# Products of the identity in TensorE's first waits, and another order of the first weight conversions

## The chip, the cores and the metric

The kernel runs on one NeuronCore of one Trainium2 chip. The time is the device time of one execution in microseconds (us), as the median of several executions. TensorE (PE) multiplies matrices, ScalarE (ACT) and VectorE (DVE) work on elements, GpSimd (POOL) does some of that and issues some transfers, and SyncE (SP) issues most transfers. Each engine has its own queue; they wait for one another by semaphores.

## What is computed

A gated linear attention is followed by a bilinear feed-forward layer, all in fp32:

```
f = 1/(1+exp(-f_logit))                            # 4 batches, 8 heads, 768 steps, 48 wide
state = f[t] * state + outer(k[t], v[t])           # per batch and head
y[t] = q[t] @ state
x = y as (3072 tokens, 384)
out = ((x @ w_a) * (x @ w_b)) @ w_out              # w_a, w_b: 384 x 1536; w_out: 1536 x 384
```

The weights come as 64-bit floats, of which the kernel makes 32-bit ones on the chip.

## The kernel before, in words

**Tiling.** The tokens are cut into 8 blocks of 384. A block needs two *units* of attention (four heads each, over the block's tokens), so units 0 and 1 make block 0, units 2 and 3 make block 1. A unit passes through these steps, each a function of the kernel: `front_parts` (sigmoids on ACT, an affine step on POOL, running products on DVE, and the multiplication of k and q by them, L306 to L333), `turn` and `turned` (transposes of k on PE, L411, and their copy out of PSUM on ACT, L418 or L420), `scores` (L387) and `mask` (L400, DVE), `gains` (L435) and `carried` (L462 and L464: the states are added up on DVE), `hand_on` (L473: the last state is scaled for the next half), `within` (L484) and `across` (L510), which add both parts of y up in PSUM, and `y_of`: `out_of_bank` copies y out of PSUM in three parts (L529), and `stored` moves it by small transfers into the block's `xT` (L549).

**Feed-forward.** For the first two blocks, `up(blk, i)` multiplies one 128-wide tile of w_b and then of w_a by the block (L593: three products for each, into two PSUM banks). I call this a *tile pair*, and its halves b and a. `product` copies b out on ACT (L613) and multiplies it by a on DVE (L615), which gives both banks back. There are four such banks, `ps_f`, handed out in turn by the list `idle`. So a tile pair can start only when the product before the last one has been taken out. After 24 tile pairs come the products with w_out (L808), and for later blocks other forms of the same (L715); these last stages are written out by a planner from estimated durations.

**Weights.** `load_weights` loads piece after piece (SP); pieces 2j and 2j+1 hold two tiles of w_b and of w_a (pieces 0, 1, 12 and 13 one tile; 14 to 19 are w_out). `begin` and `end` convert them by a generator in three steps: two ACT operations and one on POOL (L58, L59, L60), two more on ACT (L62, L63), and one plus one on DVE (L68, L73; the latter three times, once for each 128 rows, for w_a and w_b). `begin(n)` carries pieces up to n through the ACT steps, `begin(n + 0.5)` only the first of these for one more piece; `end(n)` carries them through all. `needed(i)` says how many pieces tile i needs; tile 7 needs pieces 8 and 9.

**Order.** Everything before the planner is written out by hand, in the function's text, in the order in which each engine's queue then has it. Each engine takes its own instructions in that order. The text goes through units 0 and 1, block 0's first tile pairs mixed with units 2 and 3, and then a loop over `ups`, which mixes the two blocks' tile pairs and converts one more piece with each. The planner begins with the last of these tile pairs, and puts the attention of unit 4 and later beside the main work.

Of the kernel before, what the change touches and what calls it, by code (L numbers as in the profile page):

```python
# [136 lines left out]
def by_quotients(ctx, tc, q, k, f_logit, v, moe_w_a, moe_w_b, moe_w_out, out, ident, weights, bad):  # L137
    nc = tc.nc
# [3 lines left out]
    NKT, NFT, DM = w_ba.shape[2], w_out.shape[1], out.shape[1]  # L142
    NH = S // BLK
    NQ = H // 4
    NC = BLK // C
    NJ = BLK // SUB
# [5 lines left out]
    FIRST = range(NQ)  # L152
# [46 lines left out]
    def load_unit(u, names="fkqv"):  # L199
        for do in loads_of(u, names):  # L200
            do()
# [37 lines left out]
    def load_weights(n=1):  # L239
        for _ in range(n):  # L240
            if len(raws) == len(todo):
                return
            dst, src, (k, m) = todo[len(raws)]
            raw = dst
            if src.dtype != FP32:

                if len(raws) in EARLY:
                    raw = groups[:, EARLY.index(len(raws))].bitcast(mybir.dt.uint64)
                else:
                    raw = next(raw_places)  # L250
                raw = raw[:, 0:k * m].rearrange("p (k m) -> p k m", k=k)
            nc.sync.dma_start(out=raw, in_=src)
            raws.append(raw)

    def begin(n):

        while 2 * n > begun[0] < 2 * len(todo):
            i, second = divmod(begun[0], 2)
            dst, src, shape = todo[i]
            if not second:  # L260
                going.append(
                    from_double(
                        nc, dst, raws[i], shape[0], next(blocks), bits[i % len(bits)], sign, whole, shape[0] == NKT
                    )
                    if src.dtype != FP32 else iter(())
                )
            next(going[i], None)
            begun[0] += 1

    def end(n):  # L270

        while ended[0] < min(n, len(todo)):
            begin(ended[0] + 1)
            next(going[ended[0]], None)
            ended[0] += 1
            if ended[0] > 2 and ended[0] - 1 not in EARLY:
                load_weights()
# [15 lines left out]
    def halves(x):  # L293
        return x.rearrange("p n s -> p (n s)")
# [56 lines left out]
    ps_f = [ps_a.tile([128, 512], FP32, tag=f"ps_f{i}", name=f"ps_f{i}") for i in range(4)]  # L351
    idle = list(range(4))
# [14 lines left out]
    def home(u):  # L367

        return ps_y if u in (1, 3) else ps_x
# [25 lines left out]
    def mask(u):  # L395

        at = sb1.tile([128, 2, BLK], FP32, tag="at", name="at")
        to, x = (y.rearrange("s h (o t) -> s h o t", t=SUB) for y in (at, home(u)[:, :, 0:BLK]))
        tri = causal.unsqueeze(1).unsqueeze(1)
        nc.vector.tensor_tensor(to, x, tri.broadcast_to((128, 2, 2 * NC, SUB)), ALU.mult)  # L400
        live[u]["at"] = at

    def turn(u):

        kf = halves(sets[u % NSET]["k"])
        live.setdefault(u, {})["kT"] = sb1.tile([128, 2, NC, 128], FP32, tag="kT", name="kT")
        ps = live[u]["turned"] = [ps_f[idle.pop(0)] for _ in range(2)] if u in FIRST else pair_of(away(u))
        for n in range(2):
            for c in range(NC):
                o = n * BLK + c * C  # L410
                nc.tensor.transpose(ps[n][:, c * C:c * C + C], kf[:, o:o + C], ident)  # L411
# [10 lines left out]
    def gains(u, chunks=range(NC)):  # L422

        _, half, _ = unit(u)
        t, kT = sets[u % NSET], live[u]["kT"]
        last = half == NH - 1
        ps = live[u]["turned"]
        for n in range(2):
            for c in chunks:
                for p in range(2):  # L430
                    if last and c == NC - 1 and p == 1:
                        continue
                    for h in range(2):
                        r = slice(SUB * p, SUB * p + SUB)
                        nc.tensor.matmul(  # L435
                            ps[p][R * h:R * h + D, (n * NC + c) * D:(n * NC + c) * D + D],
                            lhsT=kT[r, n, c, R * h:R * h + D],
                            rhs=t["v"][r, n, c, h * D:h * D + D],
                            start=True,
                            stop=True,  # L440
                        )
        if chunks[0]:
            return
        st = sb3.tile([128, NJ, 2, D], FP32, tag="st", name="st")
        before = live[u - NQ]["st"][NJ] if half else None
        live[u]["st"] = [before] + [st[:, j] for j in range(NJ - 1 if last else NJ)]

    def carried(u, js=range(NJ)):

        for j in js:  # L450
            if j + 1 < len(live[u]["st"]):
                carry(u, j)
        if js[-1] == NJ - 1:
            give_back(live[u]["turned"])
# [11 lines left out]
    def hand_on(u):  # L466

        if unit(u)[1] == NH - 1:
            return
        before = live[u]["st"][-1]  # L470
        for n in range(2):
            end = products_of_f[u][:, n, BLK - 1:BLK]
            nc.vector.tensor_scalar(before[:, n], before[:, n], end, math.exp(-MIDDLE), ALU.mult, ALU.mult)  # L473
# [45 lines left out]
    def out_of_bank(u, part):  # L519

        if not part:
            if u == NQ - 1:

                live[u]["y_sb"] = groups[:, 2 * NTG - 1, PIECE:].rearrange("r (o p m) -> r o p m", p=2, m=SUB)
            else:
                live[u]["y_sb"] = sb1.tile([128, 2 * NC, 2, SUB], FP32, tag="y", name="y")
        p, e, r, rows = ((0, 0, 0, 128), (1, R, 0, D), (1, 0, R, D))[part]
        copy = nc.vector.tensor_copy if u in FIRST and p else nc.scalar.copy
        copy(live[u]["y_sb"][r:r + rows, :, p], live[u]["y"][p][e:e + rows, 0:BLK].rearrange("r (o m) -> r o m", m=SUB))  # L529

    def stored(u):
# [49 lines left out]
    def up(blk, ft):  # L581

        for _, _, _, do, *args in up_steps(blk, ft):
            do(*args)
# [22 lines left out]
    def product():  # L607

        if not factors:
            return  # L610
        blk, ft, ps = factors.pop(0)
        b_sb = next(b_copies)
        nc.scalar.copy(b_sb, ps["b"][:, 0:BLK])  # L613
        a, b = (x.rearrange("p (g t) -> p g t", g=NTG) for x in (ps["a"][:, 0:BLK], b_sb))
        nc.vector.tensor_tensor(products(blk)[:, :, ft], a, b, ALU.mult)  # L615
        give_back(ps.values())
# [321 lines left out]
    with tc.manual_schedule():  # L938
# [11 lines left out]
        def emit_all(steps):  # L950
            for _, _, do, *args in steps:
                do(*args)

        def y_of(u):
            for part in range(3):
                out_of_bank(u, part)
            stored(u)
# [16 lines left out]
        for _ in range(3):  # L974
            next(fronts[0])
        begin(1)
        turn(0)
        turned(0)
        scores(0)
        begin(2)  # L980
        gains(0)
        for _ in range(3):
            next(fronts[1])
        turn(1)
# [15 lines left out]
        within(1)  # L1000
        gains(1, range(NC - 1, NC))
        across(0)
        carried(1, range(1, 5))
        for u in FIRST:
            if u:
                across(u)
# [3 lines left out]
            stored(u)  # L1010
        begin(3)
        end(2)
        for u in FIRST:
            carried(u, range(5, NJ))
        emit_all([*scans, *others[0]])


        load_unit(3, "f")
        load_unit(2, "v")
        load_weights()  # L1020
        load_unit(3, "k")
        load_unit(3, "q")
        load_unit(3, "v")
        load_weights()
        up(0, 0)
        emit_all(others[1])
        begin(4)
        next(fronts[3])
        end(4)
        for u in FIRST:  # L1030
            hand_on(u)
        turn(2)
        scores(2)
        load_unit(4, "f")
        up(0, 1)
        mask(2)
        product()
        turned(2)
        begin(5)
# [3 lines left out]
        gains(2)  # L1043
        product()
        carried(2)
        begin(6)
        up(0, 2)
        across(2)
        end(5)
# [2 lines left out]
        y_of(2)  # L1052
        load_weights(2)
        product()
        up(0, 3)
        turn(3)
        turned(3)
        scores(3)
        begin(7)
        mask(3)  # L1060
        up(0, 4)
        product()
        begin(8)
        within(3)
        gains(3)
        carried(3)
        product()
        end(7)
        begin(9)
        end(8)  # L1070
        across(3)
        y_of(3)


        ups = [(0, 5), (0, 6)]
        for i in range(7, NFT):
            ups += [(1, i - 7), (0, i)]
        ups += [(1, i) for i in range(NFT - 7, NFT)]
        alone = len(todo) - 6
        for n, (blk, i) in enumerate(ups[0:alone]):  # L1080
            convert(needed(i))
            up(blk, i)
            end(7 + n)
            product()
            begin(ended[0] + 2)
            if 2 < n < 2 + 2 * NSET and n % 2:
                load_unit(NSET + n // 2, "kqv" if n == 3 else "fkqv")
# [523 lines left out]
```

## Time and profile before

| | |
|---|---|
| runs | 606.65, 605.12, 606.56 us; median 606.56 us |
| profiled execution | 605.75 us, of which the span from first to last instruction is 604.0 us |
| mean granted TensorE clock | 0.987 |
| PE busy | 571.5 us (95%) |
| DVE busy | 412.9 us (68%) |
| ACT busy | 267.9 us (44%) |
| POOL busy | 76.6 us (13%) |

Busy shares are of the span. A plain fp32 product stands as two matmul records in the trace, a transpose as one; a record's duration includes the time in which it runs beside its neighbours, so the spacing of starts is the better measure of speed. The granted clock is the share of full speed that the throttle let TensorE have. Waits are named by the engine that ended them.

### The profile page before, as it was taken

What the parts mean: (1) busy time and instruction counts of PE and PEld (TensorE: products, weight loads), DVE (VectorE), ACT (ScalarE), POOL (GpSimd) and SP (SyncE); (2) the same over time, 40 slices, a digit from 0 to 9 for tenths busy, and PEclk for the clock granted to TensorE, in tenths of its full rate; (3) what the DMA queues carried; (4) which work ended last, traced back from release to release, by engine and by line L of the source; (5) the groups of instructions that cost most, each with busy time, mean ns of one, the idle gap of its engine ahead of it and who ended that gap; (6) DMA issues with size and microseconds to landing.
All of it is one profiled execution on the core that took longest, in us unless ns stands there. A gap on an engine that the chain in (4) does not pass through costs nothing.

```text
span 604.0 us, 13895 instructions
## 1 busy us (share of the span) xinstructions
PE 571.5 (95%) x5778; PEld 512.5 (85%) x5778; DVE 412.9 (68%) x788; ACT 267.9 (44%) x505; POOL 76.6 (13%) x71
## 2 busy tenths in 40 slices
PE   1689799999999999999999999999999999999995
PEld 1546455557899999999989999999999999999995
DVE  6897444589968778967895768846775165746741
ACT  6476878963232455326521354326331335134300
POOL 6252433534200000000000000000000000000000
PEclk9979799999999999999999999999999999999999
DMA  9695579159743333045003420022001100000000
GB/s 207 186 276 158 186 206 297 71 90 173 142 126 105 84 77 67 2 105 119 3 1 84 117 51 2 1 78 68 2 2 47 47 0 1 2 27 0 1 29 31
DMA packets 33272, 49.42 MB, mean 82 GB/s; under 512 B 3952, under 2 KB 24976, under 8 KB 33200
## 3 DMA queue, kind: packets, MB, share of 16 engines
q1 hardware_dynamic: 30000, 42.38, 25.9%
q0 software_dynamic: 3056, 5.92, 5.8%
q8 instruction: 47, 0.77, 0.6%
q14 instruction: 25, 0.20, 0.1%
q10 hardware_dynamic: 144, 0.15, 0.1%
HBM read 33.23 MB, written 4.72 MB: 63 GB/s over the span
## 4 chain that ended last, share of the span: by engine, by line
PE 87%; DVE 7%; issue 2%; ACT 2%; DMA 1%; SPq 0%; DVEq 0%; ACTq 0%
PE ps_f L715 35%; PE ps_f L808 28%; PE ps_f L593 16%; PE ps_y L484 2%; PE ps_x L387 2%; PE ps_y L510 2%; PE ps_x L411 1%; PE ps_x L435 1%; DVE inv L329 1%; DVE sums L707 1%; DVE groups L707 1%; DVE groups L316 1%; DMA f_in<-in_f_logit_dram 1%; DVE q_in L333 1%; DMA xT<-y 1%
## 5 line engine op out<-in xcount | busy, mean ns | idle before, releaser
L593 PE MATMUL ps_f<-xT,w_ba 128*128 128x384 f32 x288 | 101.2, 511 | 6.9 <-DMA xT<-y 4.7
L593 PEld LDWEIGHTS ps_f<-xT,w_ba 128*128 128x128 f32 x288 | 56.3, 199 | 47.0 <-issue 9.5
L1259 ACT COPY sums<-ps_f 128x384 f32<-128x384 f32 x120 | 57.5, 480 | 75.9 <-PE ps_f L715 68.2
L1259 ACT COPY groups<-ps_f 128x384 f32<-128x384 f32 x120 | 57.7, 481 | 62.9 <-PE ps_f L715 39.9
L715 PE MATMUL ps_f<-xT,w_ba 128*128 128x192 f32 x384 | 78.4, 327 | 0.0
L715 PEld LDWEIGHTS ps_f<-xT,w_ba 128*128 128x128 f32 x384 | 64.8, 190 | 0.2
L715 PE MATMUL ps_f<-groups,w_ba 128*128 128x192 f32 x288 | 55.5, 327 | 0.0
L715 PE MATMUL ps_f<-x_sums,raw 128*128 128x192 f32 x288 | 54.0, 331 | 1.2 <-DVE groups L707 0.9
L808 PE MATMUL ps_f<-w_out,sums 128*128 128x192 f32 x288 | 52.2, 329 | 0.0
L808 PE MATMUL ps_f<-w_out,groups 128*128 128x192 f32 x288 | 51.7, 328 | 0.0
L715 PEld LDWEIGHTS ps_f<-x_sums,raw 128*128 128x128 f32 x288 | 46.9, 190 | 4.3 <-DVE groups L707 1.8
L808 PE MATMUL ps_f<-spare,sums 128*128 128x192 f32 x288 | 49.0, 326 | 0.0
L715 PEld LDWEIGHTS ps_f<-groups,w_ba 128*128 128x128 f32 x288 | 47.9, 190 | 0.5 <-ACT groups L1259 0.3
L808 PEld LDWEIGHTS ps_f<-w_out,sums 128*128 128x128 f32 x288 | 47.1, 190 | 0.8 <-DVE o L843 0.3
L808 PEld LDWEIGHTS ps_f<-w_out,groups 128*128 128x128 f32 x288 | 47.1, 190 | 0.7
L808 PEld LDWEIGHTS ps_f<-spare,sums 128*128 128x128 f32 x288 | 47.1, 190 | 0.1
L60 POOL TENSOR_SCALAR sums<-sums 128x768 f32<-128x768 f32 (+1 forms) x20 | 39.9, 1994 | 53.6 <-ACT sums L58 53.6
L312 POOL TENSOR_SCALAR inv<-inv 128x768 f32<-128x768 f32 x14 | 12.8, 912 | 266.7 <-ACT inv L309 266.6
L707 DVE TENSOR_TENSOR sums<-sums,groups 128x768 f32<-128x768 f32 x36 | 34.7, 965 | 14.2 <-ACT groups L1259 13.7
L707 DVE TENSOR_TENSOR sums<-ps_f,sums 128x384 f32<-128x384 f32 x60 | 32.8, 553 | 16.5 <-PE ps_f L715 15.0
L715 PE MATMUL ps_f<-x_sums,w_ba 128*128 128x192 f32 x192 | 39.3, 327 | 0.5 <-DVE sums L707 0.5
L715 PE MATMUL ps_f<-xT,raw 128*128 128x192 f32 x192 | 39.4, 328 | 0.0
(135 smaller groups left out, 857.9 us busy)
## 6 DMA issues: line engine op xcount, KB each, us to landing
raw<-w_ba POOLq DMA_DIRECT2D x11, 512.0 KB, 8.0
k_in<-in_k_dram SPq DMA_DIRECT2D x32, 144.0 KB, 3.9
q_in<-in_q_dram SPq DMA_DIRECT2D x32, 144.0 KB, 4.4
v_in<-in_v_dram SPq DMA_DIRECT2D x16, 288.0 KB, 5.0
raw<-in_moe_w_out_dram SPq DMA_DIRECT2D x6, 768.0 KB, 6.3
out_dram<-o SPq DMA_DIRECT2D x24, 192.0 KB, 1.9
f_in<-in_f_logit_dram SPq DMA_DIRECT2D x28, 144.0 KB, 3.1
xT<-y SPq DMA_DIRECT2D x45, 72.0 KB, 2.2
```

What stands on the lines that cost most here:

```text
L60: nc.gpsimd.tensor_scalar(h, h, HI_MAX, None, ALU.min)
L312: nc.gpsimd.tensor_scalar(inv, inv, EXP_K, 1.0, ALU.mult, ALU.add)
L316: nc.vector.tensor_tensor_scan(F[:, c], F[:, c], none, math.exp(MIDDLE), ALU.mult, ALU.add)
L329: nc.vector.tensor_tensor_scan(inv[:, w], inv[:, w], none[:, 0:C], first, ALU.mult, ALU.add)
L387: nc.tensor.matmul(ps[h][SUB * p:SUB * p + SUB, o:o + SUB], lhsT=kf[r, tokens(n, c, p)], rhs=qf[r, tokens(n, c, p)], start=True, stop=True,)
L484: nc.tensor.matmul(ps[p][e:e + D, o:o + SUB], lhsT=t["v"][r, n, c, h * D:h * D + D], rhs=at[r, h, o:o + SUB], start=o == 0, stop=True, ski ...
L510: nc.tensor.matmul(ps[p][e:e + D, o:o + SUB], lhsT=st[j][r, n], rhs=qf[r, tokens(n, c, p)], start=False, stop=True, skip_group_check=True,)
L593: nc.tensor.matmul(ps[nm][:, 0:BLK], lhsT=w[:, kt, ft * 128:ft * 128 + 128], rhs=xT[blk][:, kt], start=kt == 0, stop=kt == NKT - 1,)
L707: nc.vector.tensor_tensor(to, x, y, op)
L715: nc.tensor.matmul(ps[:, g], lhsT=sums_of_w[name][:, g, 128 * j:128 * j + 128], rhs=sums_of_x[blk][name], start=start and g == 0, stop=Tru ...
L808: nc.tensor.matmul(to, lhsT=x[:, i // 2, i % 2], rhs=w[:, NI * (i % 2) + i // 2], start=start and i == 0, stop=i == HFT - 1, skip_group_ch ...
L1259: do(*args)
```

## The change

Four things change.

1. A new function `keep_up(n)` makes n products of the identity with itself, 128 x 128, into the PSUM bank that stands last in `idle`. Nobody reads them. They stand on TensorE's queue three times: 9 before unit 0's transposes, 12 after unit 0's `gains`, and 30 before block 0's first tile pair.
2. Unit 0's second and third part of y are copied by ACT and no longer by DVE; unit 1's stay on DVE. DVE adds up the last states of units 0 and 1, and does the second of unit 2's first running products, before unit 1's copies and no longer after them.
3. Loads and conversions come in another order at units 2 and 3: pieces 4 and 5 are loaded earlier, unit 3's v later; `mask(2)` comes before `hand_on`; the first ACT steps of pieces 6, 7 and 8 come before ACT work that stood ahead of them or follow it more closely.
4. Tile pair (0, 4) still comes before `within(3)`, but (0, 5), which was the loop's first, now stands between `gains(3)` and `across(3)`. The loop over `ups` goes (0, 6), (0, 7), (1, 0), (0, 8), (1, 1) and so on, where it went (0, 5), (0, 6), (1, 0), (0, 7), (1, 1); the planner gets the last four tile pairs where it had five.

```diff
-        copy = nc.vector.tensor_copy if u in FIRST and p else nc.scalar.copy
+        copy = nc.vector.tensor_copy if u == NQ - 1 and p else nc.scalar.copy
...
+        def keep_up(n):
+
+            for _ in range(n):
+                nc.tensor.matmul(ps_f[idle[-1]][:, 0:128], lhsT=ident, rhs=ident, start=True, stop=True)
...
         begin(1)
+        keep_up(9)
         turn(0)
...
         gains(0)
+        keep_up(12)
         for _ in range(3):
             next(fronts[1])
...
         across(0)
-        carried(1, range(1, 5))
+        carried(1, range(1, NJ))
+        carried(0, range(5, NJ))
+        emit_all(scans)
...
         end(2)
-        for u in FIRST:
-            carried(u, range(5, NJ))
-        emit_all([*scans, *others[0]])
+        emit_all(others[0])
 
         load_unit(3, "f")
+        load_weights()
         load_unit(2, "v")
         load_weights()
         load_unit(3, "k")
         load_unit(3, "q")
-        load_unit(3, "v")
-        load_weights()
+        keep_up(30)
         up(0, 0)
         emit_all(others[1])
         begin(4)
         next(fronts[3])
+        end(3)
+        load_unit(3, "v")
         end(4)
-        for u in FIRST:
-            hand_on(u)
         turn(2)
         scores(2)
         load_unit(4, "f")
         up(0, 1)
         mask(2)
+        for u in FIRST:
+            hand_on(u)
         product()
...
-        begin(6)
+        begin(6.5)
         up(0, 2)
         across(2)
...
         product()
+        begin(7.5)
         up(0, 3)
         turn(3)
         turned(3)
         scores(3)
-        begin(7)
+        end(7)
         mask(3)
-        up(0, 4)
         product()
         begin(8)
+        up(0, 4)
         within(3)
         gains(3)
+        end(8)
         carried(3)
         product()
-        end(7)
-        begin(9)
-        end(8)
+        begin(8.5)
+        up(0, 5)
         across(3)
         y_of(3)
+        begin(9)
+        product()
 
-        ups = [(0, 5), (0, 6)]
-        for i in range(7, NFT):
-            ups += [(1, i - 7), (0, i)]
-        ups += [(1, i) for i in range(NFT - 7, NFT)]
+        ups = [(0, 6), (0, 7)]
+        for i in range(8, NFT):
+            ups += [(1, i - 8), (0, i)]
+        ups += [(1, i) for i in range(NFT - 8, NFT)]
...
             up(blk, i)
-            end(7 + n)
+            end(8 + n)
             product()
```

## The prediction

> **What bounds the kernel.** I read the page's busy times and slices first.
>
> ```profile
> PE 571.5 (95%) x5778; PEld 512.5 (85%) x5778; DVE 412.9 (68%) x788; ACT 267.9 (44%) x505; POOL 76.6 (13%) x71
> ...
> PE   1689799999999999999999999999999999999995
> ...
> PEclk9979799999999999999999999999999999999999
> ```
>
> PE is the bound, and what it loses lies ahead of 70 us: of 32.5 us idle, and the clock's two dips. Next, PE's waits up to 110 us:
>
> ```profile
> PE ps_f L411 <- DVE k_in L333: 15.0, 2, 12.5
> PE ps_f L593 <- DMA xT<-y: 4.7, 1, 4.7
> PE ps_f L593 <- DVE w_ba L73: 2.2, 1, 2.2
> PE ps_y L510 <- DVE st L464: 1.5, 2, 1.2
> ```
>
> Then PE's timeline (start, us, what):
>
> ```profile
> 12.49 1.51 PE L411 MATMUL ps_f<-ident,k_in 128*128 128x128 f32 x6 [12.49 <-DVE k_in L333]
> ...
> 33.11 7.24 PE L593 MATMUL ps_f<-xT,w_ba 128*128 128x384 f32 x12 [4.74 <-DMA xT<-y]
> 40.19 0.82 PE L411 MATMUL ps_y<-ident,k_in 128*128 128x128 f32 x6
> 40.94 0.93 PE L387 MATMUL ps_x<-q_in,k_in 48*64 48x64 f32 x48
> 41.79 4.14 PE L593 MATMUL ps_f<-xT,w_ba 128*128 128x384 f32 x12
> ...
> 64.67 1.16 PE L510 MATMUL ps_y<-q_in,st 48*48 48x64 f32 x48 [1.22 <-DVE st L464]
> ```
>
> The same tile pair takes 7.24 us after the wait and 4.14 later; the transposes 1.51 and 0.82. So PE runs at half speed up to about 25.5 us, from 33 to 39, and after 68. The clock row shows no dip before 30, but the durations do (L484 changes pace at 25.5). The windows agree for the later two (granted clock: third column from the right):
>
> ```profile
> 33.20:40.20 7.00, 7.00 (x13) 3.43 (x14) 6.83 (x12) 5.87 (x9) 3.92 (x3) 0.57 1.02 277
> 63.40:68.00 4.60, 1.22 (x52) 0.92 (x49) 3.36 (x9) 4.57 (x7) 2.84 (x2) 0.84 0.78 262
> 68.00:74.60 6.60, 6.60 (x13) 3.65 (x14) 2.39 (x6) 5.01 (x9) 1.91 (x2) 0.60 0.21 61
> ```
>
> After 70 PE waits for nothing over 1 us, so whatever is gained before stays, unless a new wait takes it back. ACT can: it needs 3.57 us a piece and works without a gap for long stretches.
>
> ```profile
> 80.96 0.90 ACT L58 ACTIVATE sums<-raw 128x768 f32<-128x768 f32 x1
> 81.76 0.99 ACT L59 ACTIVATE spare<-raw,whole 128x768 f32<-128x768 uint32 x1
> 82.65 0.90 ACT L62 ACTIVATE spare<-raw 128x768 bf16<-128x768 f32 x1
> 83.58 1.07 ACT L63 ACTIVATE spare<-spare 128x768 uint16<-128x768 bf16 x1
> 84.53 0.88 ACT L58 ACTIVATE sums<-raw 128x768 f32<-128x768 f32 x1
> ```
>
> [...]windows of 1 us put the dips at 32.4 to 39.2 and 66.5 to 73.3, 6.8 us each[...].
>
> **The change, part by part.**
>
> *Price of an identity product.* The trace has none. A plain fp32 product is two records; a 384-wide record at full speed follows every 0.3225 us (0.64 at half), and a 128-wide transpose record every 0.109 (0.213). I take 2 x 0.109 = 0.218 us, at half speed 0.427. Below, one record's 0.109; above, 0.427.
>
> *9 and 12 products.* The identity is built on POOL at 10.34 us. 9 x 0.427 = 3.84 puts the first transposes from 12.49 to at most 14.3. Scores and gains then end at 17.9 (16.45 before), and 12 products take 2.6 us at full and 5.1 at half speed: unit 1's transposes start between 19.0 (as before) and 21.6 by when the clock rises[...]. Behind them wait ACT's copies of kT and unit 2's sigmoid, which ended at 22.86 and is wanted by DVE at 24.58 (slack 1.7), and `mask(1)` at 23.38, whose scores ended at 22.03 (1.35). A delay of up to 1.7 costs nothing, more costs up to 0.4. Faster PE takes away DVE's 0.52 us wait for the gains at 26.05. `across(1)` ends between 27.8 and 28.7; I take 28.3 (28.37 before).
>
> *30 products.* 30 x 0.218 = 6.54: they end at 34.9. The first tile pair waited for xT until 33.11; xT comes 0.5 earlier or up to 0.3 later, hidden behind the products, which overshoot by 1.8. What they buy: 4.07 instead of 7.08 us for tile pair (0, 0) (41.79 to 45.86, against 33.11 to 40.19).
>
> *Unit 0's copies on ACT, DVE's order.* ACT gets 2 x 0.48 us, in its wait of 0.97 for unit 1 (if that were gone, y(1) would be as much later, still behind the 30 products); DVE loses 1.14 and fills its waits of 0.34 and 0.31 with 1.5 us of sums and scan. It reaches unit 2's reciprocal at 30.7, not 32.53, so k and q are ready at 34.6 and 35.5, pieces 2 and 3 by 39.7. PE wants them at 38.9 and 42.5: no wait. The store DMAs are the same; SP's begin 0.6 earlier.
>
> *Loads.* Pieces 4 and 5 are issued around 32.5 and 33.5 and land in 6.4 and 8.5 us: 39 and 42, wanted by ACT at 40 and 44.6. They come behind the xT transfers on SP. Unit 2's v (5.0) lands by 38, wanted at 44.5; unit 3's k and q by 41, wanted at 51; its v behind piece 6, wanted at 62. POOL's queue is unchanged. Nothing. If piece 4 came 1 us late, (0, 3) would, by as much.
>
> *Up to across(3).* Six tile pairs at 4.07 are 24.4. Attention, from starts in the trace: 1.60 + 1.34 + 0.82 + 1.60 + 1.4 + 1.0 = 7.8. DVE, chained from 39.7 on (mask 0.9, hand_on 0.65, product 0.5, scans 4.75, product 0.5, states 1.35, piece 4 1.65, k and q 1.75, piece 5), lets half a of (0, 3) start at 53.6 for 52.9: 0.8. 34.9 + 24.4 + 7.8 + 0.8 = 67.9. The waits of 1.22 and 2.17 and the second dip's 2.65 us are gone, since (0, 5) covers the state sums, pieces 6 and 7 are ready at 55.7 and 60.1, and PE stays busy. Before, the same work was done at 74.6: 6.7 us ahead.
>
> *What is late next.* (0, 6) ends at 71.8. (0, 7) now follows at once, and needs piece 8, which DVE takes in hand only behind the product of (0, 6): 0.3 + 0.56 + 0.55 + 0.4 makes PE wait 2.0 to 2.1, to 73.8. Half a needs piece 9: on ACT, y(3) (68.1 to 69.5), the rest of piece 8 (1.9), two product copies (0.8), piece 9 (3.6) end at 75.8, plus DVE 0.4: 76.3, a wait of 0.6. (1, 0) ends at 82.1. (0, 8) needs the banks of (0, 7), whose copy stands on ACT behind pieces 10 and 11: 75.8 + 7.1 + 0.45 = 83.4, a wait of 1.3. So (0, 8) starts at 83.4. Before, it would follow the same nine tile pairs at 68.0 + 6.6 + 3 x 3.87 = 86.2. **Gain 2.8 us.** After that ACT has slack: it catches up, by its 1.3 us gaps between product copies.
>
> *Clock after the new wait.* [...] I charge 0.2 (0 to 1.5).
>
> *The planner's part.* With the loop one tile pair longer, combining w_out and unit 4 start at the same absolute time, with PE 3 to 4 us further on. In the new order unit 4's scores stand one tile pair (3.87) later, so they come at 138 as before, where DVE had q ready at 138.0. Block 2's sums were ready at 188.5 for a start at 199.4: slack 11. I take 0 (-1 to +1.5).
>
> Sum on the profiled execution: 605.75 - 2.8 + 0.2 = **603.1 us** (span 601.4). It lies 0.8 below the median of the runs shown[...].
>
> **Rivals.** About 0.3% (1.8 us) is what a measurement tells from no change.
>
> 1. *ACT's queue doesn't hold.* The wait at (0, 8) is 1.3 or the one at (0, 7) shorter, or the planner's part gains: the 6.7 us ahead keeps 5. For it: DVE and ACT are estimated to within 1 us. Against it: the queues' order. 605.75 - 5 = 600.7. Chance 0.11.
> 2. *A new wait takes it.* A full dip at 73.5 (1.5) or a wait of PE for unit 4 to 6 on DVE, which is busy 96% from 140 to 160 (1.5): 605.75 - 2.8 + 2.5 = 605.5, no change. Chance 0.14.
> 3. *Slower.* The 30 identity products run at half speed, because they don't raise the clock or it falls before them: 12.8 us to 41.1 instead of 34.9, which moves everything behind by 6.3: 605.75 - 2.8 + 6.3 = 609.2. For it: PE had raised the clock only at 25.5[...]. Against it: plain products did raise it, before and at 39. It decides above 0.31 us a product: then (0, 0) starts after 37.7 and nothing is left of the 2.8. This is also the case that the change doesn't do what it says. Chance 0.09.
>
> The forecast has 0.66, from 601.0 to 604.6. The range of 600.8 to 606.2 leaves out rival 3 and the lower half of rival 1. Faster: 0.66 + 0.11 = 0.77; same 0.14; slower 0.09.
>
> **What would show it.** The 30 products in 6.5 us at clock 1.0; (0, 0) in 4.1 us, ahead of 36; no wait at `across(3)` or (0, 5); a new wait of 2 us for L73 at (0, 7), near 72, and one of 1.3 for ACT near 82; unit 1's transposes after 19 with the clock up before 22. Wrong would make it: products above 0.3 us each, a wait at (0, 3) over 2 us, or PE idle over 1 us more than before after 140.

## The result: no change that can be measured

The changed kernel takes 605.59 us (median; 604.71 to 609.14), the kernel before on the same chip 605.60 us (603.89 to 607.07). The ratio, which is formed from all executions and is not the quotient of the two medians, is 1.001, with a 95% interval of 0.9997 to 1.0022. The forecast of 603.1 us, 2.65 us under the profiled 605.75, was wrong. The profiled execution took 606.54 us with a span of 604.7 us, against 605.75 and 604.0 before.

The page of the changed kernel: busy times, TensorE's slices and the granted clock.

```profile
PE 577.5 (96%) x5880; PEld 521.3 (86%) x5880; DVE 411.9 (68%) x786; ACT 268.7 (44%) x507; POOL 76.3 (13%) x71
...
PE   3899989999999999999999999999999999999995
...
PEclk9799999999999999999999999999999999999998
```

PE is busy for 6.0 us more and has 102 more records, which are the 51 identity products. Its early slices are filled, but the clock row has a 7 in the second slice: a slow stretch where there was none before. The waits of PE up to 160 us (line, whom it waited for, us in total, times, longest):

```profile
PE ps_f L957 <- POOL ident masks.py:199: 10.4, 1, 10.4
PE ps_f L593 <- DVE w_ba L73: 3.6, 2, 2.4
PE ps_x L484 <- issue: 1.3, 1, 1.3
PE ps_y L484 <- DVE at L400: 0.7, 1, 0.7
PE ps_f L808 <- ACT x_sums L613: 0.6, 1, 0.6
PE ps_f L593 <- ACT x_sums L613: 0.6, 1, 0.6
PE ps_x L510 <- issue: 0.2, 1, 0.2
```

The waits for xT (4.7) and for the state sums at `across(3)` (1.2) are gone, as forecast. New are 1.3 us of "issue" (time in which the engine waited for nothing that the profile shows) in unit 0's `within`, which the forecast does not have at all, and 2.4 us for piece 8. PE's timeline (start, us, what, idle before it) shows the first of these and what comes of it:

```profile
10.38 3.88 PE L957 MATMUL ps_f<-ident 128*128 128x128 f32 x18 [10.38 <-POOL ident masks.py:199]
14.10 0.82 PE L411 MATMUL ps_f<-ident,k_in 128*128 128x128 f32 x6
...
20.67 0.55 PE L484 MATMUL ps_x<-at,v_in 64*48 64x64 f32 x23
22.53 0.59 PE L484 MATMUL ps_x<-at,v_in 64*48 64x64 f32 x25 [1.31 <-issue]
...
24.17 1.53 PE L484 MATMUL ps_y<-at,v_in 64*48 64x64 f32 x48 [0.69 <-DVE at L400]
...
29.61 7.54 PE L957 MATMUL ps_f<-ident 128*128 128x128 f32 x60
36.99 4.04 PE L593 MATMUL ps_f<-xT,w_ba 128*128 128x384 f32 x12
40.86 0.82 PE L411 MATMUL ps_y<-ident,k_in 128*128 128x128 f32 x6
```

The first transposes already run at full speed (0.82 for 1.51 us). Then PE stops in the middle of `within(0)`, between its 23rd and 24th record, for nothing that another engine owes it. The same operation for unit 1 takes 1.53 us instead of some 0.9 at full clock. Windows of the trace, cut where the clock changes (length, PE, weight loads, DVE, ACT, POOL, granted clock, DMA share, GB/s), say the rest:

```profile
13.78:24.02 10.24, 8.39 (x264) 7.62 (x263) 9.93 (x22) 7.29 (x13) 2.91 (x3) 1.00 1.03 293
24.02:30.85 6.83, 6.48 (x150) 6.12 (x151) 4.21 (x13) 1.90 (x4) 1.21 (x1) 0.50 0.05 14
30.85:36.99 6.14, 6.14 (x57) 6.14 (x56) 6.01 (x15) 4.06 (x5) 3.31 (x4) 1.00 0.71 180
66.50:73.30 6.80, 6.80 (x67) 4.08 (x66) 0.64 (x2) 3.02 (x5) 0.00 (x0) 1.00 0.16 50
```

The dips at 33 and 66 us are gone (1.00 in the last two lines); one at 24.0 to 30.8 has come. In the 3.4 us ahead of it PE was idle for 1.31 us and for the first 0.54 of the 0.69, so 46% busy.

This fall of the clock is not in most executions. Each one's mean granted clock was measured: the profiled one has 0.991, twelve of the 22 have 0.996 or 0.997, and a fall of 6.8 us takes off 0.006 (3.4 of 605 us). Those twelve have a median of 605.1 us, the seven at 0.991 or 0.992 one of 606.5, and the three at 0.986 to 0.989 one of 609.0. The mean does not tell where a fall lies. What follows is the account of the profiled execution.

**Where the time went.** Up to the tenth tile pair, which starts at 85.40 for 86.19 (it is (0, 8) in the new order and (1, 1) in the old one), PE's time divides like this (from starts in both timelines):

| us of PE ahead of the tenth tile pair | before | after | difference |
|---|---|---|---|
| idle in the three waits that the products stand in | 19.78 | 10.38 | -9.40 |
| identity products (3.72 + 2.78 + 7.38) | 0 | 13.88 | +13.88 |
| other waits | 4.13 | 6.39 | +2.26 |
| the kernel's own work | 62.28 | 54.75 | -7.53 |
| sum | 86.19 | 85.40 | -0.79 |

The kernel's own work became 7.5 us faster by the clock. To buy that, 13.9 us of products were put in, of which only 9.4 fit into idle time. Then, after 120 us, PE's waits. Of the kernel before:

```profile
PE ps_f L715 <- DVE groups L707: 0.9, 1, 0.9
PE ps_f L715 <- DVE sums L707: 0.5, 1, 0.5
PE ps_y L510 <- issue: 0.4, 1, 0.4
PE ps_f L715 <- ACT groups L1259: 0.2, 1, 0.2
```

And of the changed kernel:

```profile
PE ps_f L715 <- DVE groups L707: 1.3, 2, 0.9
PE ps_f L808 <- DVE u L837: 0.9, 1, 0.9
PE ps_f L808 <- ACT x_sums L613: 0.6, 1, 0.6
PE ps_f L715 <- ACT sums L1271: 0.5, 1, 0.5
PE ps_f L715 <- ACT groups L1271: 0.2, 1, 0.2
```

That is 3.59 us for 1.99 (single waits of 0.62, 0.47, 0.48, 0.93, 0.85 and 0.23 against 0.45, 0.46, 0.86 and 0.23): 1.60 us more, so that 0.79 ahead becomes 0.81 behind, and the spans differ by 0.7.

### The profile page after: what moved, and what is told of

It reads as the page before. It is cut to its first block, busy times and chain, and to the rows that moved or that the text cites. A ratio compares the mean times of both kernels' runs of the same rounds, so it can differ in the third digit from the quotient of the medians.

```text
span 604.7 us, 14106 instructions
## 1 busy us (share of the span) xinstructions
PE 577.5 (96%) x5880; PEld 521.3 (86%) x5880; DVE 411.9 (68%) x786; ACT 268.7 (44%) x507; POOL 76.3 (13%) x71
## 4 chain that ended last, share of the span: by engine, by line
PE 80%; DVE 11%; ACT 4%; issue 3%; DMA 1%; SPq 0%; DVEq 0%; ACTq 0%
PE ps_f L715 33%; PE ps_f L808 26%; PE ps_f L593 12%; PE ps_y L484 2%; DVE groups L707 2%; PE ps_x L387 2%; PE ps_y L510 2%; DVE sums L707 1%; DVE inv L329 1%; PE ps_x L435 1%; PE ps_f L957 1%; PE ps_x L411 1%; DVE f_in L316 1%; DVE st L464 1%; DVE spare L329 1%
## 5 line engine op out<-in xcount | busy, mean ns | idle before, releaser
L593 PE MATMUL ps_f<-xT,w_ba 128*128 128x384 f32 x288 | 96.0, 490 | 4.2 <-DVE w_ba L73 3.6
L593 PEld LDWEIGHTS ps_f<-xT,w_ba 128*128 128x128 f32 x288 | 53.6, 190 | 41.8 <-ACT spare L59 3.0
L715 PEld LDWEIGHTS ps_f<-xT,w_ba 128*128 128x128 f32 x384 | 64.7, 190 | 0.1
L707 DVE TENSOR_TENSOR sums<-sums,groups 128x768 f32<-128x768 f32 x36 | 34.9, 970 | 14.3 <-ACT groups L1271 13.9
L707 DVE TENSOR_TENSOR sums<-ps_f,sums 128x384 f32<-128x384 f32 x60 | 32.8, 552 | 15.6 <-PE ps_f L715 14.3
```

Of the source, the lines that this page charges most:

```text
L593: nc.tensor.matmul(ps[nm][:, 0:BLK], lhsT=w[:, kt, ft * 128:ft * 128 + 128], rhs=xT[blk][:, kt], start=kt == 0, stop=kt == NKT - 1,)
L707: nc.vector.tensor_tensor(to, x, y, op)
L715: nc.tensor.matmul(ps[:, g], lhsT=sums_of_w[name][:, g, 128 * j:128 * j + 128], rhs=sums_of_x[blk][name], start=start and g == 0, stop=Tru ...
```

## The experiments

Each kernel was timed beside the kernel before on the same chip; "ratio" is to that, with its 95% interval. The kernels ran on two chips, so times from different experiments are compared by their ratios. Tile pairs are written (block, tile).

### The order alone

All three `keep_up` calls are taken out of the changed kernel:

```diff
-        keep_up(9)
...
-        keep_up(12)
...
-        keep_up(30)
```

> The changed kernel without any identity product: the new order alone. Theory P (the products cost TensorE as much as they bring: 14.2 us of it, of which 9.4 lie in idle time, for 7.9 us less of slow clock; the order is worth what is left): tile pair (0, 0) starts near 33.5 us and takes 7.1 at half clock, so it ends at 40.6, within 0.4 us of the 40.9 of the changed kernel, and the time is that of the changed kernel within 1 us (604.6 to 606.6). Theory Q (the products bring their 3 us, and the new order's waits take them back): without the products the time is 2 to 3 us longer than the changed kernel's, 607.6 to 608.6.

Measured: 606.04 us, ratio 1.0019 (1.0008 to 1.0029). (0, 0) starts at 33.13 and is at half clock again, (0, 8) starts at 84.54 (85.40 in the changed kernel), and PE's later waits are those of the changed kernel. Within theory P's range, and not Q's: the products of the changed kernel bring at most about 0.1%, and the order by itself is no gain.

### The 30 products without the 9 and the 12

```diff
-        keep_up(9)
...
-        keep_up(12)
```

> The changed kernel with the 30 products, without the 9 and the 12. Theory P: units 0 and 1 run as in the kernel before, across(1) ends at 28.4 instead of 29.6 us, the 30 products end at 34.9 (6.5 us) and (0, 0) starts 2.1 us earlier than in the changed kernel (36.99); half of that or more stays: 603.5 to 604.8. Theory Q: the early products keep the clock up, so that without them the 30 begin at half clock and end at 37 or later: 605.6 or slower; and if the order's waits decide, an earlier (0, 0) only makes the wait at (0, 7) longer, 605.6.

Measured: 604.68 us, ratio 0.9997 (0.9988 to 1.0007). This is the stretch as the forecast described it, in PE's timeline:

```profile
21.46 1.43 PE L484 MATMUL ps_x<-at,v_in 64*48 64x64 f32 x48
...
27.55 6.96 PE L957 MATMUL ps_f<-ident 128*128 128x128 f32 x60
34.35 4.04 PE L593 MATMUL ps_f<-xT,w_ba 128*128 128x384 f32 x12
```

The time is within theory P's range. There is no stop in `within(0)`, the 30 products take 6.80 us from start to start, (0, 0) starts at 34.35 and (0, 8) at 83.42, where the forecast had 34.9 and 83.4. Against the order alone the 30 bring 0.22%; against the changed kernel 2.0 us at (0, 8) in the profiles and 0.13% by the ratios, whose intervals overlap. The clock fell early in this execution too, from 19.3 to 22.7 us, behind PE's wait of 2.70 us for unit 1's k; it was up again before the 30 products. The time is still that of the kernel before, since the late waits (0.62, 0.48, 0.48, 0.93) are all there.

### 20 products for 30

```diff
-        keep_up(30)
+        keep_up(20)
```

once without the 9 and the 12, and once with them:

> The changed kernel with 20 instead of 30 products, without the 9 and the 12. Theory P: 20 x 0.218 = 4.4 us from 28.4 end at 32.8, before xT is there (33.1 to 34.3), so they cost TensorE nothing; (0, 0) starts at 33.1 to 34.3 at full clock and takes 4.1, 3 us ahead of the changed kernel; with 1 us of it lost to longer waits for pieces 2 and 3: 602.9 to 604.5, and 1 us ahead of the kernel with 30 alone. Theory Q: the waits for pieces 2, 3, 4 and 8 grow by what is gained: 605.6, and no difference between 20 and 30.

> The changed kernel with 20 instead of 30 products, the 9 and the 12 kept. If the 30 run past the point where xT is there (near 35 in the changed kernel, whose (0, 0) starts at 36.99), ten fewer let (0, 0) start near 35: 1 to 2 us less than the changed kernel, ratio 0.998 to 0.9995. If xT or the pieces set the time there, nothing changes: 1.001.

Measured: 604.21 us, ratio 0.9987 (0.9976 to 0.9998), without the early ones; 605.95 us, 1.0017 (1.0008 to 1.0025), with them. The first lies in P's range, but its interval overlaps that of the 30. The second contradicts the part of theory P that blamed the overshoot: with ten products fewer (0, 0) starts at 33.32 instead of 36.99, waits for the rest of xT until 34.90, and then PE waits 1.98 us instead of 1.13 at `across(2)` and at the two halves of (0, 3). (0, 8) comes 0.7 us earlier in the profile and the median shows nothing. So the products that run past xT cost nearly nothing here: in the profile, what is earlier at (0, 0) is waited away by (0, 3), which DVE's conversions and states set.

### The products in the old order

The kernel before, with `keep_up` and its three calls in the same places:

> The kernel before with the 9, the 12 and the 30 products in the same three places, in its own order. Theory P: (0, 0) starts near 37 and takes 4.0, so it ends at 41.0 for 40.2 before; the waits of 1.22 and 2.17 us and the slow stretch after 66 stay: 605.6 to 607. Theory Q: the products bring their 3 us in this order as well, less 1 for the later start: 603 to 604.5.

Measured: 611.32 us, ratio 1.0095 (1.0074 to 1.0116). Both theories missed this by 4 us and more. The timeline of PE shows what neither had seen:

```profile
33.23 9.63 PE L957 MATMUL ps_f<-ident 128*128 128x128 f32 x60 [3.67 <-DVE st L464]
```

The products write into the bank that stands last in `idle`, and in the old order DVE reads that bank (the last states, L464) only behind unit 1's copies. The products that should fill the wait had to wait themselves, PE stood idle for 3.67 us, the clock fell at 32.0, and the 60 records ran at half speed for 5.6 of their 9.5 us: (0, 0) started at 42.70 and the tenth tile pair at 92.64, 6.45 later than before. In the changed kernel DVE's earlier `carried` frees the bank in time. The forecast had taken that move for a rearrangement of DVE's idle time alone.

### Five tile pairs to the planner

The loop ends one tile pair earlier, so that the planner gets as many as before. From there on the order of all engines' instructions is that of the kernel before.

```diff
-        alone = len(todo) - 6
+        alone = len(todo) - 7
```

once in the changed kernel, and once in that with 20 products alone:

> The changed kernel, all its products in place, with one tile pair fewer in the written loop, so that the planner gets five as in the kernel before. Theory R (0.8 us of the gain reach tile pair (0, 8) and the planner's new order loses 1.6 of it after 145 us, by TensorE's waits of 0.62, 0.48, 0.48, 0.92 and 0.85 where the kernel before has 0.45, 0.46 and 0.86): the waits are those of the kernel before again, and the profiled span falls from 604.7 by 1.1 to 1.6; median 604.0 to 604.6. Rival S (those waits only pass on what VectorE and ScalarE owe at that point, whatever the order): they come back in other places, 605.6.

> The changed kernel with 20 products alone (no 9, no 12) and five tile pairs to the planner. Theory R: 2.8 us ahead at (0, 8) (83.4 for 86.2) and no loss after 145: 605.4 - 2.6 = 602.8 (602.3 to 603.4), the forecast of 603.1 made good. Rival S: 604.2 as with 20 products and four tile pairs.

Measured: 604.04 us, ratio 0.9991 (0.9982 to 0.9999); and 603.22 us, ratio 0.9969 (0.9961 to 0.9978). Theory R holds: against the same kernel with four tile pairs the ratio is 0.19 and 0.18% lower. PE's waits after 120 us in the first of them:

```profile
PE ps_f L715 <- DVE groups L707: 0.9, 1, 0.9
PE ps_f L715 <- DVE sums L707: 0.5, 1, 0.5
PE ps_f L808 <- DVE groups L615: 0.3, 1, 0.3
PE ps_f L715 <- ACT groups L1271: 0.2, 1, 0.2
PE ps_f L808 <- DVE o L843: 0.2, 1, 0.2
```

The waits for `u`, for ACT's `sums` and for `x_sums` are gone: 2.03 us in all instead of 3.59. Without the early products, with 20 for 30, and with five tile pairs, the time is 603.22 us. That is the forecast's number but not its gain: the kernel before took 604.95 us beside it, so 0.31% was gained where 0.44% (2.65 us) had been forecast.

### What the early products set off

The 12 left out, the 9 and the 30 kept:

```diff
-        keep_up(12)
```

> The changed kernel with the 9 and the 30 products, without the 12. If it is the sum of early products that leads to TensorE's stop of 1.3 us in unit 0's within (seen with 9 and 12, in neither kernel without them), half as many leave none or a shorter one, and (0, 0) starts at 34.3 to 35.5: 604.5 to 605.2, near the 604.7 of 30 alone. If 9 alone bring it, (0, 0) starts near 37 as in the changed kernel: 605.6.

Measured: 605.24 us, ratio 1.0011 (1.0001 to 1.0021), like the changed kernel, and 0.14% over the 30 alone. The stop of `within(0)` is there, 1.39 us, so it does not take the 12. In this profiled execution the clock stayed up all the same and (0, 0) started at 34.54; its time of 604.58 was near the lowest of that kernel. Four of its 19 executions have a mean clock of 0.997 or 0.998, as this one, and a median of 604.8 us; eight have 0.992 and 606.0. So the executions with the lower clock took 1.2 us more.

The stop has a fixed place in the count of TensorE's instructions, not in the work. It comes behind 449 of them (221 products' records, the weight loads, and 7 others) in the changed kernel, in that with five tile pairs, in the old order with products, in that with 9, 12 and 20, and in that with 9 and 30. In the kernels without the 9, PE passes that place at 22.9 to 23.4 us and does not stop. So the number of instructions was made the variable, with the time on TensorE nearly unchanged:

```diff
-            for _ in range(n):
-                nc.tensor.matmul(ps_f[idle[-1]][:, 0:128], lhsT=ident, rhs=ident, start=True, stop=True)
+            for _ in range(n // 3):
+                nc.tensor.matmul(
+                    ps_f[idle[-1]][:, 0:BLK].rearrange("p (n m) -> p n m", n=3),
+                    lhsT=ident,
+                    rhs=ident.unsqueeze(1).broadcast_to((128, 3, 128)),
+                    start=True,
+                    stop=True,
+                )
```

> The changed kernel with each three identity products made one product of 384 columns (the identity repeated three times as the moving operand): 3, 4 and 10 products, 34 records instead of 102, for the same time on TensorE (34 records of 0.3225 us are 11.0 at full clock, 102 of 0.109 are 11.1). Theory F (TensorE's stop of 1.1 to 1.8 us comes behind its 221st record in all four kernels with the 9[...]): 28 records fewer lie ahead of that point, which moves from within(0) to within(1), and it is reached later than 22.7, so the stop falls to 0 to 0.4; across(1) ends at 28.3 to 28.8 instead of 29.6, (0, 0) starts at 34.5 to 35.5 instead of 36.99, and the time is 1 to 2 us under the changed kernel's (ratio to before 0.998 to 1.000). Rival G (the stop belongs to the early work of TensorE, not to its number of instructions): it stays in within(0) with over 1 us, and the time is the changed kernel's (1.001).

Measured: 605.42 us, ratio 1.0006 (0.9996 to 1.0015). PE's timeline:

```profile
20.93 0.85 PE L484 MATMUL ps_x<-at,v_in 64*48 64x64 f32 x48
21.60 0.25 PE L435 MATMUL ps_f<-v_in,kT 64*48 64x48 f32 x2
22.89 0.57 PE L435 MATMUL ps_f<-v_in,kT 64*48 64x48 f32 x30 [1.04 <-issue]
```

`within(0)` now runs through, and the stop comes 27 records later in the work, in the gains of unit 1. That is again behind exactly 449 instructions of TensorE. So the stop goes with the number of instructions, as theory F has it, and G falls. F's size was wrong: PE reached the place at 21.85 instead of after 22.7, so 1.04 us of the stop remained, the clock fell at 24.8, (0, 0) started at 36.89, and the time cannot be told from the changed kernel's.

### Pieces 8 and 9 ahead of y(3)

This starts from the kernel with 20 products and five tile pairs and goes for the wait at (0, 7). In the changed kernel that wait looks like this on ACT, DVE and PE:

```profile
70.19 1.46 ACT L529 COPY y<-ps_y 128x384 f32<-128x384 f32 x3 [6.02 <-PE ps_y L510]
71.68 0.90 ACT L62 ACTIVATE spare<-raw 128x768 bf16<-128x768 f32 x1
72.60 1.06 ACT L63 ACTIVATE spare<-spare 128x768 uint16<-128x768 bf16 x1
73.54 0.83 ACT L613 COPY x_sums<-ps_f 128x384 f32<-128x384 f32 x2
74.02 1.02 DVE L615 TENSOR_TENSOR groups<-ps_f,x_sums 128x384 f32<-128x384 f32 x2 [6.88 <-ACT x_sums L613]
...
75.54 1.59 DVE L73 CUSTOM_DVE_ANT_0 w_ba<-sums,spare 128x512 uint16<-128x512 uint16 x3
...
76.61 8.17 PE L593 MATMUL ps_f<-xT,w_ba 128*128 128x384 f32 x24 [2.44 <-DVE w_ba L73]
```

ACT stands idle for 6.02 us with the rest of piece 8 (L62, L63) behind the copies of y(3), which wait for `across(3)`; DVE for 6.88 us behind ACT. First piece 8 is moved:

```diff
-        begin(8.5)
+        begin(9)
         up(0, 5)
         across(3)
         y_of(3)
-        begin(9)
+        end(9)
         product()
+        begin(10)
```

> The kernel with 20 products and five tile pairs to the planner, with piece 8's second ScalarE step ahead of across(3) (ScalarE stands idle there for 6 us) and its VectorE step ahead of the product of (0, 5), and piece 9 begun right behind that product. Theory R: the wait of 2.44 us at (0, 7) falls to 0 to 0.5: 600.6 to 601.2, 2 us under the kernel with 20 and five. Rival S: ScalarE's queue is full from 67 on, so the wait moves to (0, 8) or (0, 9) and 0 to 0.5 us is left of it.

Measured: 602.91 us, ratio 0.9951 (0.9932 to 0.9970). (0, 7) now follows (0, 6) at once, but stops in its second half, for piece 9, for 2.10 us; the clock dips from 76.3 to 79.7. The ratio is 0.18% lower than without the move, but its interval takes that one in. Three of the seven executions took 600.6 to 601.3 us, as theory R said to within 0.1, and four 602.9 to 603.4, near rival S; what divides them is not known. Then piece 9 as well:

```diff
         begin(9)
+        begin(10)
         up(0, 5)
         across(3)
         y_of(3)
         end(9)
         product()
-        begin(10)
+        end(10)
```

> As with piece 8 ahead, and piece 9's four ScalarE operations moved ahead of the copies of y(3) as well, into the 4.1 us that ScalarE still stands idle there, with VectorE's step behind the product that precedes them. Theory R: the wait of 2.10 us in the second half of (0, 7) falls to 0 to 0.4: 600.3 to 601.5, ratio 0.992 to 0.994. Rival S: the pieces behind come no earlier, since ScalarE has no idle time after 69, and the wait moves to (0, 8) or (0, 9): 602.5 to 603, ratio 0.995 as before it.

Measured: **599.43 us, ratio 0.9908 (0.9891 to 0.9925)**, 5.7 us under the kernel before on the same chip (605.17) and faster than both kernels of this study. Its timeline around the same place:

```profile
64.92 0.90 ACT L62 ACTIVATE spare<-raw 128x768 bf16<-128x768 f32 x1
65.85 1.08 ACT L63 ACTIVATE spare<-spare 128x768 uint16<-128x768 bf16 x1
66.50 0.89 PE L510 MATMUL ps_y<-q_in,st 48*48 48x64 f32 x48
67.32 12.85 PE L593 MATMUL ps_f<-xT,w_ba 128*128 128x384 f32 x39
67.48 1.46 ACT L529 COPY y<-ps_y 128x384 f32<-128x384 f32 x3 [0.55 <-PE ps_y L510]
```

ACT's idle time ahead of y(3) is down from 6.02 to 0.55 us, and PE runs from 67.32 without a wait. (0, 8) starts at 79.03, 4.2 us ahead of the kernel with piece 8 alone: most of it is the wait of 2.10 us and some 1.7 for the 3.4 us at half clock that followed it, both gone. Theory R had counted the wait only, so the measured time (of five executions) lies below its range.

Finally the same without any identity product:

```diff
-        keep_up(20)
```

> As with pieces 8 and 9 ahead and five tile pairs to the planner, without the 20 identity products: no identity product is left. If the products keep the clock up in TensorE's wait for xT, as the runs with the unimproved order say (20 products took 0.32% off the order alone, 1.0019 to 0.9987), (0, 0) again takes 7 to 8 us at half clock and the time is 1.9 us over the 599.4 of the same order with 20: 601.3, ratio 0.993 to 0.995. If the order has made that wait harmless, 599.4 stays, ratio 0.991.

Measured: 599.86 us, ratio 0.9920 (0.9903 to 0.9937). The two intervals overlap. The clock falls at 32.1 again, and from (0, 0) to (0, 1) it takes 8.74 us for 6.43 with the 20. (0, 8) starts 1.8 us later than with them, but at the end of the span 1.0 is left. So of the 0.9% nearly all is the order, with the two conversions and the five tile pairs; what the products add is 0.1%, too little to be told from nothing here.

## Why the prediction was wrong

Step by step, with the forecast's own numbers.

- **Price of an identity product: right.** 0.218 us at full speed and 0.427 at half were taken. 30 take 6.80 us from start to start where the clock is up (0.227 each), and the 9 took 3.72 (0.413), nearly all of it at half speed.
- **9 and 12 products: this step failed.** Unit 0's transposes start at 14.10 ("at most 14.3") and unit 1's at 19.03 ("19.0 to 21.6"), and the clock, whose rise was only estimated in the forecast, rises sooner, at 13.78. But "a delay of up to 1.7 costs nothing" looked at who waits for PE, and not at what PE itself waits for. The 9 products bring TensorE to the end of its first 449 instructions by 21.2 us (23.4 in the kernel before), and there it stops for 1.31 us, until 22.53; in the profiled execution the clock also fell at the end of the 3.4 us with this stop in them. `across(1)` ends at 29.6 instead of 28.3, and the first 1.2 us of the 30 products run at half speed. The other early kernels show both outcomes: the stop is always there with the 9, the fall of the clock is not. By the ratios the 9 and the 12 cost 0.13% beside 30 products and 0.30% beside 20.
- **30 products: right in kind, late in time.** They were to end at 34.9, and (0, 0) started at 36.99: 1.3 from the later start and 0.8 from the time they take. Without the 9 and the 12 it was 34.35. What they buy is as forecast: (0, 0) in 3.87 us instead of 7.08.
- **DVE's order: incomplete.** DVE reached unit 2's reciprocal at 32.57 instead of 30.7, since unit 0's y came late; without the 9 and the 12 it got there at 30.43. No wait came of it. What the step did not see is that it frees the products' PSUM bank; in the old order, where it doesn't, the products cost 6.5 us at the tenth tile pair.
- **Up to across(3): right, with some luck.** From (0, 0) to (0, 6) the forecast had 33.0 us (34.9 to 67.9), the trace 33.04 (36.99 to 70.03). The wait at (0, 3) was 1.13 for 0.8 and attention took 7.55 for 7.8, which cancels; the waits at `across(3)` and (0, 5) and the second dip are gone.
- **What is late next: right in mechanism, sizes off both ways.** (0, 7) waits 2.44 us for 2.0 to 2.1 (the four terms given for it make only 1.81); half a doesn't wait at all (0.6 forecast), and (0, 8) waits 0.62 instead of 1.3. Without the 9 and the 12, (0, 8) starts at 83.42, for 83.4 forecast. The clock after this wait stayed up in the changed kernel. With the 30 alone it fell for 3.4 us from 73.9 on; from (0, 7) to (0, 8) that took 9.47 us for 8.79 in the changed kernel, 0.7 more, where the forecast's estimate had charged 0.2.
- **The planner's part: this step failed too.** "I take 0 (-1 to +1.5)"; it lost 1.60, just outside. The forecast's own sign of being wrong, PE idle over 1 us more than before after 140, came true. The argument was that unit 4 and the sums of w_out begin no later than before. They begin 3.2 us later (scores at 141.2 instead of 138.0), but that isn't what costs: in the kernels that are 2.8 us ahead the waits are the same. It is the order that the planner writes when it starts with four tile pairs instead of five. Giving it five takes these waits away (2.03 us in all) and 0.19% off the ratio.

Both failures together are most of the miss. In the profiles they are 2.0 us at (0, 8) and 1.60 after it, where the forecast and the balance lie 3.4 apart (2.65 ahead, 0.8 behind). By the ratios the miss is 0.54% (1.001 for 603.1/605.75 = 0.9956). The kernel with both undone, which also has 20 products for 30, is at 0.9969 and so wins back 0.41%; the rest is not accounted for. That it took 603.22 us, next to the 603.1 of the forecast, is luck, since the kernel before was faster beside it than when it was profiled. Of the rivals, the second (605.5, a new wait takes it) has the number, but named other places for it. The third, products at half speed, is what happened in the old order, and for 1.2 us here.

What stays open: why the planner's order with four tile pairs is worse, beyond the waits it shows; and how much of what the early products cost is the stop and how much the fall of the clock. The mean clocks of the changed kernel say that both count (605.1 us in the twelve executions with the highest clock, 606.5 in the next seven), but not where in an execution the clock fell.

## What to carry to other kernels

Filler products on TensorE brought little here: of the 7.5 us that the clock gave up to the tenth tile pair, 4.5 went on products beyond the idle time and 2.3 on other waits. Before using them, see what TensorE will wait for next, see that the bank they write is free by then (PE waited 3.67 us for it in the old order), and look for new stops of TensorE itself (1.31 us behind its first 449 instructions here). Look first for an engine that stands idle with ready work queued behind a waiting instruction: moving two conversions ahead of ACT's 6 us wait was worth 0.6%, where the products at their best brought 0.1 to 0.3%. Where a written order is handed to a planner, compare the order that it writes before and after the change, before that part is costed at nothing.

## What the runs showed of the hardware that was not expected

**TensorE's "issue" waits came at fixed counts of its instructions.** The stops come behind 449 instructions of TensorE in all six kernels with the 9 (1.31 us in the changed kernel, 1.04 in that with wide products). The changed kernel stops again behind 705, 256 further on (0.20 us), and that with wide products 128 matmul records after its first stop (0.25 us). The wait of 0.45 us in the kernel before, which ends at 157.88 in unit 4's attention, comes behind 2753, which is 449 + 9 x 256. The page of the changed kernel has a queue of instructions (packets, MB, share of the DMA engines' time):

```profile
q8 instruction: 48, 0.79, 0.6%
```

These are transfers of 16 KB. The stops behind 449 and 705 in the changed kernel and the one behind 2753 in the kernel before end 2.5 to 2.7 us after one of them starts (22.53 after 19.89, 26.63 after 23.92, 157.88 after 155.40). No run moved a transfer, so what TensorE waits for in these stops was not shown; nor what starts the first transfer, at 20.22 in the kernel before, where PE has started 108 matmul records by then, and at 19.89 in the changed one, where it has started 154.

**The clock fell behind windows in which TensorE was busy for 0 to 46%.** In the profiles of the kernel before (from 25.5 us on) and of the changed kernel (from 13.8 on) the granted clock stays the same for 6.83, 6.83, 27.31, 6.83 and 529.07 us, and for 10.24, 6.83 and 570.03. All of these are multiples of 3.41 us, so that both traces can be cut into windows of that length. Up to 590 us three windows ended in a fall: PE was busy for 0% of the one from 28.9 to 32.4 and 45% of the one from 63.1 to 66.5 in the kernel before, and 46% of the one from 20.6 to 24.0 in the changed kernel. Of the other windows at full clock the emptiest was 59% busy (75.2 to 78.6 in the changed kernel), and no fall followed. The length of a wait alone does not tell what it costs. PE waits 2.44 us ahead of (0, 7) both in the changed kernel and in that with 20 products alone. In the first the wait lies in two windows, 69 and 59% busy, and the clock stayed up; in the second weight loads came 0.64 us apart from 75.32 to 78.52 behind it, half speed, for 0.32 between matmul records in the first.
